# Two stacked feed-forward experts on one core: the planned steps of expert 1 tied to the round ahead of them, chunk 2 joined to the first half of f

## The chip, the cores and the metric

One core of a Trainium2 chip runs the whole program. The metric is the device time of that core in microseconds (us); before the change three runs gave 991.14, 992.07 and 993.05, median 992.07. The profiled execution took 988.78 us, and the span of its trace is 987.0 us.

## The reference, cut to what matters

A two-dimensional DFT (sequence of 3008, width 256) keeps the real part; its 6016 rows go through two feed-forward layers of 2048 hidden units, each without bias:

```python
X = np.fft.fft(np.fft.fft(x, axis=1), axis=2).real      # (2, 3008, 256) -> 6016 rows
h = x @ moe_w_in;  g = h * (1 / (1 + np.exp(-h)))       # expert 1: SiLU
x = g @ moe_w_out
h = x @ moe2_w_in; g = np.maximum(h, 0) + alpha * np.minimum(h, 0)   # expert 2
return g @ moe2_w_out
```

## The kernel before

**Tiling.** A row k of the DFT and its mirrored row -k share their even and odd parts, so each batch is 3 chunks of 502 pairs (CW), 6 chunks in all. A chunk's input is the tile eo (even and odd part, each split into a high and a low fp32r half: product = hi·hi + lo·hi + hi·lo) and n (column 128). Chunks 0 to 2 are batch 0, chunks 3 to 5 batch 1. The 2048 hidden units are 16 slices f of 128.

**Rounds of expert 1.** `ORDER` (L49, L50) lists 96 pairs (chunk, f). Round i (L904 to L909) does, in program order:

- `eo_mm(i)`: 6 matmuls of 502 columns on TensorE into pe and po (L560 to L562); they share four PSUM buffers with the chunk work;
- `mm2(i-2)`: 12 matmuls of the round two back into four accumulators a1 (L608 hi·gh, L610 hi·gl, L612 lo·gh);
- `silu_split(i)`: on VectorE t = n·w + pe (L568), hp = t + po (L571), t = t - po (L572); on ScalarE four SiLUs (L575 gives the rounded gh, L576 the exact value); and `low1(i-1)`, the low halves gl = exact - gh (L588). gl of t is always made on GpSimd; gl of hp on GpSimd in rounds under `LO_POOL` = 17 and in rounds 52 to 87 (`lo_pool`), else on VectorE;
- the steps that `PLAN` puts at round i.

Where the list moves to another chunk, the four accumulators go to the tile o1 of their chunk (L619, L621); the second time a chunk comes, they are added to it (L617).

**Planned steps.** `PLAN` (L26 to L32) gives each piece of other work a range of rounds, and `put` spreads its steps over it: weights of f slices 4 to 15 (`i1`, `i2`, `i3` for w_in, `o0` to `o3` for w_out; f group g needs i*g* at its first `eo_mm` and o*g* at its first `mm2`), chunks 1 and 2 (`c1`, `c2`), the constants `cx` and `fa`, the second batch's first DFT stage (`x` loads, `a` folds and matmuls, `y` loads, `c3` to `c5`), and expert 2's weights (`w2`, `ws`, `wo`, and the coefficients `co` from alpha, L479 to L488, planned at round 60). A weight arrives as float64 bits; one half of 512 columns is converted by one ScalarE step (L181) and four VectorE steps (L185, L189, L193, L197), then summed (L425, L428) and split (L432, L435, L450, L454) on ScalarE and GpSimd.

**What sets the order.** Up to L840 and from L911 the order is as written. In between, a scheduler orders each engine's queue from the program order, the dependences and its own model of the times: where it believes an engine idle, it puts a ready step ahead of the round's work, however late `PLAN` has it. Each engine and the DMA queue (SyncE) then run their queues strictly in order. `tc.issue_after(ins)` binds the instructions traced inside it that are on the engine of `ins` to stand behind `ins` in that queue; it adds no wait between engines. Before the change the steps of `fa`, `o0`, `i1` and `c1` have such a bound (`behind`, L864), the others none.

Expert 2 (from L911) takes 48 steps n of 33 matmuls, in an order that is written out.

Of the kernel before, what the change touches and what calls it, by code (L numbers as in the profile page):

```python
# [15 lines left out]
ALU = mybir.AluOpType  # L16
# [39 lines left out]
A_WARM = (0, 1, 0, 1, 0, 0, 0, 0)  # L56
A_VEC = lambda b, h, i: b and h and i == 0
W2_ORDER = (0, 2, 4, 5, 1, 3, 6, 7)
LO_POOL = 17
K_PARTS = (0, 12, 24, 32)  # L60
B_GROUPS = (0, 3, 6, 9, 12, 16)
PAIRS = [(k0 + i, k0 + (k1 - k0) // 2 + i) for k0, k1 in zip(K_PARTS, K_PARTS[1:]) for i in range((k1 - k0) // 2)]
# [57 lines left out]
def fft_moe_kernel(  # L120
# [294 lines left out]
    def load_o1(g):  # L415
        load_raw(f"o{g}", wo1[:, 1024 * g : 1024 * g + 1024])
# [135 lines left out]
    def eo_mm(i):  # L552
        c, f = ORDER[i]
        g, fo = divmod(f, 4)
        sl = slice(fo * 128, fo * 128 + 128)
        eo = EO[c]
        pe, po = mm_ps(f"pe{i}", CW), mm_ps(f"po{i}", CW)
        for ps, j in ((pe, 0), (po, 2)):
            hi, lo = WI[1, g, j][:, sl], WI[1, g, j + 1][:, sl]
            nc.tensor.matmul(ps, hi, eo[:, j, :], start=True, stop=False)  # L560
            nc.tensor.matmul(ps, lo, eo[:, j, :], start=False, stop=False)  # L561
            LAST["pe"] = nc.tensor.matmul(ps, hi, eo[:, j + 1, :], start=False, stop=True)  # L562
        return pe, po

    def silu_split(i, pe, po):
        c, f = ORDER[i]
        t = work(F32, f"t{i}")
        nc.vector.scalar_tensor_tensor(t, E128[c], w128_sb[:, f : f + 1], pe, op0=ALU.mult, op1=ALU.add)  # L568
        low1(i - 1)
        hp = work(F32, f"hp{i}")  # L570
        nc.vector.tensor_tensor(hp, t, po, op=ALU.add)  # L571
        LAST["t", i] = nc.vector.tensor_tensor(t, t, po, op=ALU.subtract)  # L572
        for s, h in ((0, hp), (1, t)):
            hi = work(F32R, f"gh{i}_{s}")
            nc.scalar.activation(hi, h, AF.Silu)  # L575
# [209 lines left out]
    if True:  # L785
# [99 lines left out]
        put(*PLAN["x"], [lambda j=j: load_x(1, j, 1) for j in range(len(PIECES) - 1)])
        put(*PLAN["a"], a1)
        bs = [stage_b(1, mh) for mh in range(2)]
        for c in range(NCB):
            put(*PLAN[f"y{c}"], [lambda mh=mh, c=c: load_y(1, mh, c) for mh in range(2)])
            put(*PLAN[f"c{3 + c}"], chunk_steps(1, c, bs))  # L890
        a, b = PLAN["w2"]
        for n, j in enumerate(W2_ORDER):
            steps = [lambda j=j: load_w2(j)] + staged([(conv_w2(j, h), []) for h in range(2)])
            put(a + (b - a) * n // 8, a + (b - a) * (n + 1) // 8, steps)
        put(*PLAN["co"], [coefficients])
        for pg in range(2):
            steps = prep_ws(pg)
# [111 lines left out]
```

## Time and profile before

| | us |
|---|---|
| median of 3 runs | 992.07 |
| profiled execution | 988.78 |
| its span | 987.0 |
| PE busy | 957.1 |
| DVE busy | 775.7 |
| ACT busy | 710.4 |
| POOL busy | 405.3 |

PE is TensorE, PEld its weight loads, DVE VectorE, ACT ScalarE, POOL GpSimd, SP SyncE. The stretch to about 30 us is the first DFT stage of batch 0; expert 1 runs from there to about 480 us, expert 2 to the end. PE's ends are modelled, so two neighbouring matmuls overlap on the page; their starts are what tells their pace. PEclk is the share of the full TensorE clock (2.4 GHz) that was granted; 0.5 is 1.2 GHz.

### The profile page before, as it was taken

To read this page: it belongs to the slowest core of one execution; us is meant where nothing else is said; L and a number is where in the kernel's file an instruction comes from. 1 tells how busy PE (TensorE), PEld (TensorE's weight loads), DVE (VectorE), ACT (ScalarE), POOL (GpSimd) and SP (SyncE) were. 2 spreads that over 40 slices of the span, in tenths; PEclk is the share of its full clock that TensorE was granted. 3 is DMA by queue.
4 is the path that set the end of the run, shared out by engine and by line. 5 is a ranking of instruction groups with operands and counts; after the bars stand their busy time and mean duration, and the time that the engine had idled before them with its cause. 6 is when DMAs were issued, how large, how long until landed. Compare 5 with 4: busy or idle time off the path is not lost.

```text
span 987.0 us, 14377 instructions
## 1 busy us (share of the span) xinstructions
PE 957.1 (97%) x5186; PEld 822.9 (83%) x5186; DVE 775.7 (79%) x1328; ACT 710.4 (72%) x1410; POOL 405.3 (41%) x355
## 2 busy tenths in 40 slices
PE   9599899999999999999999999999999999999998
PEld 6478787888888788778789999999999999989997
DVE  6669898785797887777587887878878788787876
ACT  3366666655666766667888888878888788787875
POOL 3577879233347475788441221312213122131200
PEclk9899999999999999999999999999999999999999
DMA  8821100150110120100000000000000000000000
GB/s 276 280 92 59 43 0 1 40 159 1 43 43 2 58 86 1 43 0 1 1 2 22 1 22 22 1 22 1 22 12 11 22 1 22 1 22 22 1 22 21
DMA packets 16614, 37.05 MB, mean 38 GB/s; under 512 B 1824, under 2 KB 11296, under 8 KB 14880
## 3 DMA queue, kind: packets, MB, share of 16 engines
q1 hardware_dynamic: 16544, 36.15, 10.9%
q8 instruction: 40, 0.66, 0.3%
q14 instruction: 30, 0.25, 0.1%
HBM read 26.83 MB, written 9.31 MB: 37 GB/s over the span
## 4 chain that ended last, share of the span: by engine, by line
PE 82%; DVE 6%; POOL 3%; issue 3%; DMA 3%; ACT 2%; SPq 0%; DVEq 0%; POOLq 0%; ACTq 0%
PE a L768 27%; PE ac L670 20%; PE a L610 7%; PE a L608 6%; PE a L612 6%; PE b L670 3%; PE pe L560 2%; PE pe L562 2%; PE po L560 2%; PE pe L561 2%; PE po L562 2%; PE po L561 2%; DMA ys<-ya 2%; PE psa L281 1%; POOL gl L588 1%
## 5 line engine op out<-in xcount | busy, mean ns | idle before, releaser
L768 PE MATMUL a<-gh,wo 128*128 128x502 f32 x768 | 268.4, 391 | 0.0
L588 POOL TENSOR_TENSOR gl<-t,gh 128x502 fp32r<-128x502 f32 x96 | 129.6, 1350 | 91.9 <-ACT t L576 65.4
L768 PEld LDWEIGHTS a<-gh,wo 128*128 128x128 f32 x768 | 145.1, 189 | 23.0
L610 PE MATMUL a<-gl,wo 128*128 128x502 f32 x384 | 150.1, 396 | 10.4 <-POOL gl L588 10.4
L737 DVE SCALAR_TENSOR_TENSOR h<-h,fc,q 128x502 f32<-128x502 f32 x192 | 129.7, 675 | 38.2 <-ACT q L732 35.3
L768 PE MATMUL a<-gl,wo 128*128 128x502 f32 x384 | 149.7, 391 | 0.0
L612 PE MATMUL a<-gh,wo 128*128 128x502 f32 x384 | 148.5, 393 | 0.0
L748 DVE TENSOR_TENSOR gl<-h,gh 128x502 fp32r<-128x502 f32 x192 | 140.7, 733 | 0.1
L575 ACT ACTIVATE gh<-hp 128x502 fp32r<-128x502 f32 x96 | 59.8, 623 | 104.5 <-DVE hp L571 102.1
L608 PE MATMUL a<-gh,wo 128*128 128x502 f32 x384 | 123.7, 397 | 6.4 <-ACT gh L575 6.4
L743 ACT ACTIVATE gh<-h 128x502 fp32r<-128x502 f32 x192 | 118.4, 617 | 2.1 <-DVE h L737 2.1
L732 ACT ACTIVATE q<-h,fc 128x502 f32<-128x502 f32 x192 | 116.9, 609 | 2.9 <-DVE h L715 1.5
L610 PEld LDWEIGHTS a<-gl,wo 128*128 128x128 f32 x384 | 73.0, 190 | 27.7 <-POOL gl L588 13.1
L646 POOL TENSOR_TENSOR xt<-o 128x252 f32<-128x252 f32 x24 | 16.6, 713 | 187.1 <-ACT q L732 131.0
L608 PEld LDWEIGHTS a<-gh,wo 128*128 128x128 f32 x384 | 71.7, 191 | 23.2 <-ACT gh L575 9.4
L588 POOL TENSOR_TENSOR gl<-hp,gh 128x502 fp32r<-128x502 f32 x52 | 68.9, 1324 | 49.2 <-ACT hp L576 44.4
L571 DVE TENSOR_TENSOR hp<-t,po 128x502 f32<-128x502 f32 x96 | 64.5, 672 | 27.2 <-PE po L562 23.7
L568 DVE SCALAR_TENSOR_TENSOR t<-n,sm,pe 128x502 f32<-128x502 f32 x96 | 70.2, 731 | 19.4 <-PE pe L562 16.5
L612 PEld LDWEIGHTS a<-gh,wo 128*128 128x128 f32 x384 | 73.0, 190 | 14.6
L768 PEld LDWEIGHTS a<-gl,wo 128*128 128x128 f32 x384 | 72.6, 189 | 7.7
L704 ACT ACTIVATE u<-ac 128x252 f32<-128x252 f32 x96 | 36.6, 381 | 52.5 <-PE ac L670 52.5
L656 POOL TENSOR_TENSOR os<-o,os 128x252 fp32r<-128x252 f32 x36 | 32.3, 910 | 95.8 <-ACT os L655 92.8
(191 smaller groups left out, 2291.9 us busy)
## 6 DMA issues: line engine op xcount, KB each, us to landing
out_t<-ot SPq DMA_DIRECT2D x24, 251.0 KB, 2.6
x<-in_xs SPq DMA_DIRECT2D x8, 512.0 KB, 5.2
raw_i<-in_wi SPq DMA_DIRECT2D x8, 512.0 KB, 7.5
raw_w<-in_wi SPq DMA_DIRECT2D x4, 1024.0 KB, 6.3
raw_w<-in_wo SPq DMA_DIRECT2D x4, 1024.0 KB, 4.9
raw_o<-in_wo SPq DMA_DIRECT2D x3, 1024.0 KB, 4.9
y<-ys SPq DMA_DIRECT2D x16, 144.0 KB, 3.3
x<-in_xs SPq DMA_DIRECT2D x2, 1024.0 KB, 5.0
```

Of the source, the lines that this page charges most:

```text
L568: nc.vector.scalar_tensor_tensor(t, E128[c], w128_sb[:, f : f + 1], pe, op0=ALU.mult, op1=ALU.add)
L571: nc.vector.tensor_tensor(hp, t, po, op=ALU.add)
L588: (nc.gpsimd if s or lo_pool(i + 1) else nc.vector).tensor_tensor(lo, h, hi.bitcast(F32), op=ALU.subtract)
L608: nc.tensor.matmul(ACC1[lb, s], hi, G[i, s][0], start=st, stop=False)
L610: nc.tensor.matmul(ACC1[lb, s], hi, G[i, s][1], start=False, stop=False)
L612: nc.tensor.matmul(ACC1[lb, s], lo, G[i, s][0], start=False, stop=sp)
L670: nc.tensor.matmul(to, w, x, start=start and q == 0, stop=q == 2, skip_group_check=True)
L732: nc.scalar.activation(h["q", i][:, to], source(n, part), AF.Abs, scale=coef(n, i, 1))
L737: nc.vector.scalar_tensor_tensor(h[f"h{i}"][:, to], source(n, part), coef(n, i, 0), h["q", i][:, to], op0=ALU.mult, op1=ALU.add)
L743: nc.scalar.activation(hi, H[n][f"h{i}"], AF.Copy)
L748: nc.vector.tensor_tensor(lo, H[n][f"h{i}"], G[n, i][0].bitcast(F32), op=ALU.subtract)
L768: nc.tensor.matmul(ACC2[lb], w[lb][j], x, start=st and first, stop=sp and last)
```

## The change

- `behind` goes; `leash(i, steps)` takes its place for all planned steps of round i: each instruction stands, on its engine, behind the last of the round's work: t of round i-1 on VectorE (L572), the gl of round i-2 (L588, on GpSimd), the last SiLU of round i-1 (L576, ScalarE), and the last `eo_mm` matmul of round i-1 (TensorE). SyncE is not bound.
- `ORDER` takes chunks 0, 1 and 2 through f 0 to 7 and then through f 8 to 15; before, chunk 2 ran through all 16 after the other two. f slices 8 to 15 are needed at round 24 and not 16, chunk 2 at round 16 and not 32; and chunk 2's accumulators go out twice (four adds more on VectorE).
- `PLAN` has other rounds, loads of weights, x and `w2` are steps of their own, ahead of their conversions, and `a` comes in four groups of three steps.
- `LO_POOL` is 30: gl of hp moves from VectorE to GpSimd in 13 rounds.

```diff
-    "o0": (1, 2), "i1": (2, 4), "o1": (2, 5), "c1": (2, 6), "i2": (12, 16), "o2": (8, 9), "i3": (16, 18), "o3": (17, 19),
+    "o0": (1, 2), "i1": (1, 4), "o1": (4, 6), "c1": (4, 8), "cx": (8, 9), "c2": (9, 15),
 ...
-ORDER = [(c, f) for f0, f1 in zip(F_PARTS, F_PARTS[1:]) for c in range(2) for f in range(f0, f1)]
-ORDER += [(c, f) for c in range(2, NC) for f in range(NF)]
+ORDER = [(c, f) for f0, f1 in zip(F_PARTS, F_PARTS[1:]) for c in range(NCB) for f in range(f0, f1)]
+ORDER += [(c, f) for c in range(NCB, NC) for f in range(NF)]
 ...
-LO_POOL = 17
+LO_POOL = 30
 ...
-        def behind(st, *at):
+        def leash(i, steps):
+
             with ExitStack() as stack:
-                for k in at:
-                    stack.enter_context(tc.issue_after(LAST[k].ins))
-                run([st])
+                for k in (("t", i - 1), ("gl", i - 2), ("si", i - 1), ("pe", i - 1)):
+                    if k in LAST:
+                        stack.enter_context(tc.issue_after(LAST[k].ins))
+                run(steps)
 ...
         for g in (2, 3):
-            put(*PLAN[f"i{g}"], [lambda g=g: load_w1(g)] + staged(prep_w1(g)))
-            put(*PLAN[f"o{g}"], [lambda g=g: load_o1(g)] + staged(prep_o1(g)))
+            for k, load, prep in (("i", load_w1, prep_w1), ("o", load_o1, prep_o1)):
+                put(*PLAN[f"l{k}{g}"], [lambda load=load, g=g: load(g)])
+                put(*PLAN[f"{k}{g}"], staged(prep(g)))
 ...
-            run(plan.pop(i, []))
+            leash(i, plan.pop(i, []))
```

What the queues hold now, at three places. In the names, gl0_1 is round 0, half 1 (half 0 is of hp, half 1 of t); the last number is a serial; lines after the change are 2 to 4 higher.

GpSimd at the start of the rounds, before: fc is the coefficients (they read alpha's row of sm), wo1_0_1 and wo1_1_1 low halves of w_out.

```order
L454 TENSOR_TENSOR wo1_0_1_292<-cvo0_0_251,wo1_0_0_291 128x512
L483 TENSOR_SCALAR fc_83<-sm_81 128x16
L484 TENSOR_SCALAR fc_83<-sm_81 128x16
L485 TENSOR_SCALAR fc_83<-fc_83 128x16
L454 TENSOR_TENSOR wo1_0_1_292<-cvo0_1_295,wo1_0_0_291 128x512
L486 TENSOR_SCALAR fc_83<-fc_83 128x16
L337 MEMSET z0_2_447 128x4
L487 TENSOR_TENSOR fc_83<-fc_83 128x16
L488 TENSOR_TENSOR fc_83<-fc_83 128x16
L588 TENSOR_TENSOR gl0_0_364<-hp0_345,gh0_0_348 128x502
L588 TENSOR_TENSOR gl0_1_366<-t0_343,gh0_1_351 128x502
```

The same place after the change:

```order
L456 TENSOR_TENSOR wo1_0_1_292<-cvo0_0_251,wo1_0_0_291 128x512
L590 TENSOR_TENSOR gl0_0_364<-hp0_345,gh0_0_348 128x502
L590 TENSOR_TENSOR gl0_1_366<-t0_343,gh0_1_351 128x502
L456 TENSOR_TENSOR wo1_0_1_292<-cvo0_1_295,wo1_0_0_291 128x512
L590 TENSOR_TENSOR gl1_0_415<-hp1_368,gh1_0_371 128x502
L590 TENSOR_TENSOR gl1_1_417<-t1_362,gh1_1_374 128x502
L427 TENSOR_TENSOR we1_436<-cvi1_0_381,cvi1_1_385 128x512
L590 TENSOR_TENSOR gl2_0_460<-hp2_419,gh2_0_422 128x502
L430 TENSOR_TENSOR cvi1_0_381<-cvi1_0_381,cvi1_1_385 128x512
L590 TENSOR_TENSOR gl2_1_462<-t2_413,gh2_1_425 128x502
```

The six coefficient instructions are gone from here (they stand behind gl of rounds 58 and 59), and the second wo1_0_1 is behind both gl of round 0.

VectorE where weight i3 is converted, before (round 12):

```order
L568 SCALAR_TENSOR_TENSOR t12_880<-n0_1_611,sm_81,pe12_860 128x502
L185 TENSOR_SCALAR cvi3_0_1078<-cvi3_0_1078 128x512
L189 TENSOR_SCALAR cvi3_0_1078<-cvi3_0_1078 128x512
L185 TENSOR_SCALAR cvi3_1_1082<-cvi3_1_1082 128x512
L193 SCALAR_TENSOR_TENSOR cvi3_0_1078<-raw_i3_1075,cvi3_0_1078 128x512
L571 TENSOR_TENSOR hp12_886<-t12_880,po12_861 128x502
```

After the change (rounds 19 and 20):

```order
L573 TENSOR_TENSOR hp19_1205<-t19_1199,po19_1180 128x502
L187 TENSOR_SCALAR cvi3_0_1214<-cvi3_0_1214 128x512
L574 TENSOR_TENSOR t19_1199<-t19_1199,po19_1180 128x502
L187 TENSOR_SCALAR cvi3_1_1218<-cvi3_1_1218 128x512
L191 TENSOR_SCALAR cvi3_0_1214<-cvi3_0_1214 128x512
L195 SCALAR_TENSOR_TENSOR cvi3_0_1214<-raw_i3_1011,cvi3_0_1214 128x512
L570 SCALAR_TENSOR_TENSOR t20_1242<-n0_2_1002,sm_81,pe20_1222 128x502
L199 SCALAR_TENSOR_TENSOR cvi3_0_1214<-raw_i3_1011,cvi3_0_1214 128x512
L573 TENSOR_TENSOR hp20_1248<-t20_1242,po20_1223 128x502
```

Four conversion steps stood between t and hp of one round; now one does, and the others stand behind hp.

GpSimd in the last rounds of expert 1 (ws is expert 2's first weight, os0 its split input), before:

```order
L588 TENSOR_TENSOR gl92_1_4322<-t92_4278,gh92_1_4290 128x502
L656 TENSOR_TENSOR os0_1_4295<-xt0_1_4254,os0_0_4294 128x504
L588 TENSOR_TENSOR gl93_1_4365<-t93_4318,gh93_1_4330 128x502
L588 TENSOR_TENSOR gl94_1_4408<-t94_4361,gh94_1_4373 128x502
L588 TENSOR_TENSOR gl95_1_4424<-t95_4404,gh95_1_4416 128x502
```

After the change:

```order
L590 TENSOR_TENSOR gl92_1_4330<-t92_4286,gh92_1_4298 128x502
L523 TENSOR_TENSOR v2w_1_3354<-v2w_1_3354 128x512
L518 TENSOR_TENSOR ws1_5l_4342<-v2w_1_3354,ws1_5h_4341 128x512
L660 TENSOR_TENSOR os0_1_4303<-o1_0_741,os0_0_4302 128x252 x2
L590 TENSOR_TENSOR gl93_1_4373<-t93_4326,gh93_1_4338 128x502
L518 TENSOR_TENSOR ws1_7l_4386<-v2w_1_3354,ws1_7h_4385 128x512
L660 TENSOR_TENSOR os0_1_4303<-xt0_0_4261,os0_0_4302 128x504
L660 TENSOR_TENSOR os0_1_4303<-xt0_1_4262,os0_0_4302 128x504
L590 TENSOR_TENSOR gl94_1_4416<-t94_4369,gh94_1_4381 128x502
L590 TENSOR_TENSOR gl95_1_4432<-t95_4412,gh95_1_4424 128x502
```

Seven steps, most of which stood in earlier rounds, are now between the gl of rounds 92 and 94, where one stood.

## Rows read from the trace of the kernel before

**Rows 1.** The page: busy us (share of the span) and instructions.

```profile
PE 957.1 (97%) x5186; PEld 822.9 (83%) x5186; DVE 775.7 (79%) x1328; ACT 710.4 (72%) x1410; POOL 405.3 (41%) x355
```

**Rows 2.** Windows: stretch, its length, busy us (instructions) by engine, PEclk, DMA.

```profile
30.00:70.00 40.00, 28.72 (x118) 21.98 (x117) 26.32 (x48) 19.62 (x40) 26.03 (x24) 0.87 0.49 168
...
100.00:115.00 15.00, 12.19 (x55) 9.33 (x54) 14.53 (x17) 6.89 (x14) 12.42 (x9) 0.89 0.22 70
...
150.00:170.00 20.00, 19.00 (x81) 14.87 (x80) 18.44 (x24) 13.46 (x24) 20.00 (x22) 1.00 0.00 1
...
285.00:340.00 55.00, 52.88 (x239) 42.40 (x237) 46.09 (x70) 35.42 (x67) 33.55 (x27) 1.00 0.14 46
...
385.00:440.00 55.00, 51.60 (x223) 41.36 (x223) 44.25 (x62) 35.24 (x63) 40.64 (x34) 1.00 0.06 20
...
475.00:500.00 25.00, 22.88 (x138) 19.56 (x137) 14.60 (x29) 21.41 (x47) 12.88 (x12) 1.00 0.00 1
...
500.00:985.00 485.00, 482.51 (x3061) 436.89 (x3060) 388.92 (x744) 390.30 (x820) 98.47 (x97) 1.00 0.04 14
```

**Rows 3.** Timeline of TensorE: start, us, what, [idle before <-releaser].

```profile
46.33 0.79 PE L610 MATMUL a<-gl,wo 128*128 128x502 f32 x1 [7.93 <-POOL gl L588]
...
107.35 1.05 PE L608 MATMUL a<-gh,wo 128*128 128x502 f32 x2 [2.81 <-ACT gh L575]
```

**Rows 4.** Timeline of GpSimd, 39 to 46 us.

```profile
39.14 1.76 POOL L483 TENSOR_SCALAR fc<-sm 128x16 f32<-128x16 f32 x1 [9.25 <-DMA sm<-in_alpha]
...
41.29 3.06 POOL L454 TENSOR_TENSOR wo<-cvo,wo 128x512 fp32r<-128x512 f32 x1
...
45.03 1.24 POOL L588 TENSOR_TENSOR gl<-hp,gh 128x502 fp32r<-128x502 f32 x1
```

**Rows 5.** Windows where the granted clock was lower.

```profile
46.30:52.90 6.60, 6.57 (x20) 5.38 (x21) 2.83 (x4) 3.09 (x6) 3.07 (x3) 0.50 0.69 279
...
107.50:111.00 3.50, 3.50 (x8) 2.16 (x9) 3.50 (x5) 2.36 (x5) 2.97 (x3) 0.51 0.00 0
```

**Rows 6.** Timeline of TensorE at full pace, 467 to 469.4 us.

```profile
467.10 0.39 PE L610 MATMUL a<-gl,wo 128*128 128x502 f32 x1
...
469.38 0.40 PE L612 MATMUL a<-gh,wo 128*128 128x502 f32 x1
```

**Rows 7.** Groups by line and form, VectorE, 30 to 145 us: xcount, busy us, mean ns.

```profile
L568 DVE SCALAR_TENSOR_TENSOR t<-n,sm,pe 128x502 f32<-128x502 f32 x22 | 16.1, 731 | 1.3 <-PE pe L562 0.7 <-POOL gl L588 0.6
L571 DVE TENSOR_TENSOR hp<-t,po 128x502 f32<-128x502 f32 x22 | 14.8, 671 | 5.1 <-PE po L562 3.9 <-PE a L610 0.5
L572 DVE TENSOR_TENSOR t<-t,po 128x502 f32<-128x502 f32 x21 | 14.1, 673 | 0.4
L197 DVE SCALAR_TENSOR_TENSOR cvi<-raw_i,cvi 128x512 uint32<-128x512 uint32 x6 | 7.2, 1206 | 0.0
L193 DVE SCALAR_TENSOR_TENSOR cvi<-raw_i,cvi 128x512 uint32<-128x512 uint32 x6 | 6.9, 1166 | 0.0
...
L189 DVE TENSOR_SCALAR cvi<-cvi 128x512 uint32<-128x512 uint32 x6 | 4.9, 838 | 0.0
L185 DVE TENSOR_SCALAR cvi<-cvi 128x512 f32<-128x512 f32 x6 | 4.3, 728 | 0.1
```

**Rows 8.** Lines L185 and L193: ns least/median/most, first and last start.

```profile
L185 DVE TENSOR_SCALAR cvi<-cvi x8: 412/425/1500, 16.5 to 102.9; 128x512 f32<-128x512 f32 x8
...
L193 DVE SCALAR_TENSOR_TENSOR cvi<-raw_i,cvi x8: 678/691/1747, 17.4 to 108.1; 128x512 uint32<-128x512 uint32 x8
```

**Rows 9.** Timeline of VectorE, 99 to 107 us.

```profile
99.82 0.73 DVE L568 SCALAR_TENSOR_TENSOR t<-n,sm,pe 128x502 f32<-128x502 f32 x1
...
105.98 0.66 DVE L571 TENSOR_TENSOR hp<-t,po 128x502 f32<-128x502 f32 x1
```

**Rows 10.** Timeline of GpSimd, 474 to 479 us.

```profile
474.00 1.28 POOL L588 TENSOR_TENSOR gl<-t,gh 128x502 fp32r<-128x502 f32 x1 [2.46 <-ACT t L576]
477.21 1.28 POOL L588 TENSOR_TENSOR gl<-t,gh 128x502 fp32r<-128x502 f32 x1 [1.93 <-issue]
```

More of the change, by code (lines that the diff above doesn't have):

```diff
@@ L32 @@
 }
+W2_AHEAD = 2
 HALF = 252
@@ L561, in eo_mm @@
             nc.tensor.matmul(ps, lo, eo[:, j, :], start=False, stop=False)
-            LAST["pe"] = nc.tensor.matmul(ps, hi, eo[:, j + 1, :], start=False, stop=True)
+            LAST["pe", i] = nc.tensor.matmul(ps, hi, eo[:, j + 1, :], start=False, stop=True)
         return pe, po
@@ L575, in silu_split @@
             nc.scalar.activation(hi, h, AF.Silu)
-            nc.scalar.activation(h, h, AF.Silu)
+            LAST["si", i] = nc.scalar.activation(h, h, AF.Silu)
             G[i, s] = (hi, h)
@@ L587, in low1 @@
             lo = work(F32R, f"gl{i}_{s}")
-            (nc.gpsimd if s or lo_pool(i + 1) else nc.vector).tensor_tensor(lo, h, hi.bitcast(F32), op=ALU.subtract)
+            LAST["gl", i] = (nc.gpsimd if s or lo_pool(i + 1) else nc.vector).tensor_tensor(
+                lo, h, hi.bitcast(F32), op=ALU.subtract
+            )
             G[i, s] = (hi, lo)
@@ L875, in fft_moe_kernel @@
         put(*PLAN["cx"], [mixed_cosines])
-        put(*PLAN["fa"], [lambda: behind(lambda: split(fh, fl, cs[:, FA0 : FA0 + 128]), 0)])
-        put(*PLAN["o0"], [lambda st=st: behind(st, 0, ("low", 0)) for st in s1[EARLY_O0:] + p1])
-        put(*PLAN["i1"], [lambda st=st: behind(st, 0, ("t", I1_AT)) for st in staged(prep_w1(1))])
+        put(*PLAN["fa"], [lambda: split(fh, fl, cs[:, FA0 : FA0 + 128])])
+        put(*PLAN["o0"], s1[EARLY_O0:] + p1)
+        put(*PLAN["i1"], staged(prep_w1(1)))
         put(*PLAN["o1"], staged(prep_o1(1)))
-        put(*PLAN["c1"], [lambda st=st: behind(st, "pe") for st in chunk_steps(0, 1, (b00, b01))])
+        put(*PLAN["c1"], chunk_steps(0, 1, (b00, b01)))
+        put(*PLAN["c2"], chunk_steps(0, 2, (b00, b01)))
         for g in (2, 3):
-            put(*PLAN[f"i{g}"], [lambda g=g: load_w1(g)] + staged(prep_w1(g)))
-            put(*PLAN[f"o{g}"], [lambda g=g: load_o1(g)] + staged(prep_o1(g)))
-        put(*PLAN["c2"], chunk_steps(0, 2, (b00, b01)))
-        put(*PLAN["x"], [lambda j=j: load_x(1, j, 1) for j in range(len(PIECES) - 1)])
-        put(*PLAN["a"], a1)
+            for k, load, prep in (("i", load_w1, prep_w1), ("o", load_o1, prep_o1)):
+                put(*PLAN[f"l{k}{g}"], [lambda load=load, g=g: load(g)])
+                put(*PLAN[f"{k}{g}"], staged(prep(g)))
+        for j, at in enumerate(PLAN["x"]):
+            put(at, at + 1, [lambda j=j: load_x(1, j, 1)])
+        for j, at in enumerate(PLAN["a"]):
+            put(at, at + 2, a1[3 * j : 3 * j + 3])
         bs = [stage_b(1, mh) for mh in range(2)]
@@ L892, in fft_moe_kernel @@
         for n, j in enumerate(W2_ORDER):
-            steps = [lambda j=j: load_w2(j)] + staged([(conv_w2(j, h), []) for h in range(2)])
-            put(a + (b - a) * n // 8, a + (b - a) * (n + 1) // 8, steps)
+            at, to = a + (b - a) * n // 8, a + (b - a) * (n + 1) // 8
+            put(at - W2_AHEAD, at - W2_AHEAD + 1, [lambda j=j: load_w2(j)])
+            put(at, to, staged([(conv_w2(j, h), []) for h in range(2)]))
         put(*PLAN["co"], [coefficients])
```

5 rows, old and new, of the table PLAN are left out of this document.

## The prediction

> **What bounds the kernel now.** I read the busy times first, then the windows by stretch, then the two longest waits of TensorE, then the queues that ended them. TensorE is busy for 957.1 of 987.0 us [rows 1], and expert 2 leaves nothing to win: from 500 to 985 us it is busy for 482.51 of 485 [rows 2]. So only the idle time of TensorE up to 500 us can go, and the time that it spends at half its clock. The windows put that idle time into six stretches: 40 - 28.72 = 11.28 us between 30 and 70, 2.81 between 100 and 115, 1.00 between 150 and 170, 2.12 between 285 and 340, 3.40 between 385 and 440, 2.12 between 475 and 500 [rows 2]; 22.7 in all. Twice the granted clock was 0.5, its lower level of 1.2 GHz, after TensorE had stood still: while it worked for 6.57 us behind the first long wait and for 3.5 us around the second [rows 5]; half of that, 3.3 and 1.7 us, is lost. Together 27.7 us, of which the start of expert 2 (2.1) is written out by hand and not touched.
>
> The first long wait is 7.93 us, for a gl of round 0 [rows 3]. GpSimd, which makes it, stood 9.25 us for alpha's transfer in front of a coefficient that nobody needs before round 60, then did a half of w_out for 3.06 us, and only at 45.03 the gl [rows 4]. The second is 2.81 us, for a SiLU [rows 3]: VectorE began t of that round at 99.82 and hp at 105.98 [rows 9], with the four conversion steps between them that the order shows. In both, a planned step whose round lies later stands in a queue ahead of the round's own work. That is what the change forbids.
>
> **The change, part by part.** All sums are made against the profiled execution (988.78 us, 1.78 over its span); the median of the runs is 3.3 above it, and the gain is carried over to the median.
>
> *The start (30 to 70 us).* At stake are 11.28 idle and 3.3 of slow clock, 14.6 us. After the change the coefficients are no longer in front of gl, so GpSimd waits for no transfer there. What is late next is VectorE. Up to round 7 it does 8 x (0.731 + 0.671 + 0.673) = 16.6 us of t, hp and t, and the four halves of i1 and o1, each 0.728 + 0.838 + 1.166 + 1.206 = 3.94 us [rows 7], 15.8 in all: 32.4. TensorE has in the same rounds 48 matmuls of eo_mm, 72 of mm2 up to round 5 and 10 of chunk 1; ten matmuls took 469.38 - 467.10 = 2.28 us [rows 6], so 130 take 29.6. VectorE is behind by 2.8. GpSimd's queue holds 13 steps up to the gl of round 3, at some 1.26 us [rows 4, 10] 16.4 us, exactly what four rounds of 18 matmuls take: it can't catch up its late start, for which I take 2.2 (of t, hp and gl of round 0 alone, 2.6 us and the SiLUs between them, part lies beside the first eo_mm), and I add 1.4 for rounds 1 to 3, where a weight step of about 1.3 us stands ahead of a gl. That keeps 6.4 of 14.6: gain 8.2. Bounds: all 14.6; or a loss of 2, worked out under the second rival.
>
> The waits that stay are near one us each, and the clock fell only behind one of eight and one of three; so I count no slow clock there. If it falls nevertheless for as long as before, 3.3 come off.
>
> *The conversions of i2, i3, o2, o3 (100 to 115).* At stake 2.81 + 1.7 = 4.5. In the new order one conversion step stands between t and hp, not four, and the next stand behind hp, where the SiLUs hide them. I keep 0.5: gain 4.0. Bounds 0 and 4.5.
>
> *The first stage of batch 1 (150 to 170).* The folds came as one bunch; now each piece has three rounds. But two folds of 512 columns still stand behind one gl, and GpSimd was busy for all 20 us of this stretch [rows 2]. Half of the 1.0: gain 0.5, bounds 0 and 1.
>
> *Expert 2's weights (285 to 440).* At stake 2.12 + 3.40 = 5.5 of idle, the same pattern as at 100. There are 16 halves over 38 rounds, now one to four steps a round, mostly behind t or hp. VectorE's load stays: it was busy for 44.25 of 55 us [rows 2], so not every bunch can be spread. I keep 1.0: gain 4.5; bounds 5.5 and, if the steps spread over every round hold up each a little, -3.
>
> *The end of expert 1.* Between gl of rounds 92 and 94 GpSimd now has seven steps, three of them short, near 8 us, instead of one of 1.3. Before, it stood idle for 2.46 and 1.93 us here [rows 10], which covers 4.4 of the 6.7 more. The rest, 2.3, makes gl of round 94 late; its matmul comes two rounds later. I take a loss of 0.7; bounds 0 and 2.3.
>
> *Work moved.* 13 gl leave VectorE for GpSimd, four adds come for chunk 2's second exit; both lie beside a round's 4.1 us of matmuls on TensorE. GpSimd pays 13 x 1.28 us there, in rounds 17 to 29, where it has room; without that cover up to 1 us. The loads as own steps stand on SyncE, two to five rounds ahead of their readers: cost nothing, since a round is 4.1 us; a load that came late would hold VectorE's or ScalarE's head, which is the third rival.
>
> Sum: 8.2 + 4.0 + 0.5 + 4.5 - 0.7 = 16.5 us. The execution would take 972.3, the median 992.07 - 16.5 = **975.6**.
>
> *A rule against it.* VectorE's conversion steps take far longer in some places: 412 ns at least and 1500 at most for one, 678 and 1747 for another [rows 8]; and the four between t and hp of rows 9 filled 105.98 - 99.82 - 0.73 = 5.4 us. The Trainium skill, GPSIMD Engine Reference, section 1 (Specifications), says that GpSimd shares its SBUF interfaces with VectorE and that VectorE's instructions with two SBUF inputs or in a two-port mode contend with it. The trace agrees by the spread just named. By that rule alone a change that spreads conversions over rounds in which GpSimd is always at work, and moves 13 gl to it, makes VectorE slower; that is the second rival.
>
> **Rivals.**
>
> *Nearly all of it goes.* For it: the order after the change has no bunch left between t and hp, and waits under a matmul's length are hidden in the modelled ends, so more than 27.7 may be at stake. Against: VectorE's 32.4 us at the start. Then 14.6 + 4.5 + 1.0 + 5.5 = 25.6: 966.5.
>
> *VectorE slows beside GpSimd.* At the dearest price a half costs 1.5 + 1.5 + 1.75 + 1.75 = 6.5 us (rows 8's most, taken for the other two steps as well) and not 3.94; four halves cost 10.2 more, and the start loses 2. Half-way to it the start gains 3.1, and if the other gains are halved (4.5), less 0.7, 6.9 stay: 985.2. For it: the spread of rows 8, and GpSimd's queue without a gap at the start. Against: the medians, 425 and 691 ns, lie at the low end.
>
> *Slower: heads of queues.* A conversion's first step is now bound behind the last SiLU of the round before; the next, on VectorE, waits for it, and t of the next round waits behind that. There are 28 halves behind round 0. It decides at 16.5 / 28 = 0.6 us lost on TensorE for each; at 1.2 us each, one step's time [rows 7], it is 33.6 - 16.5 = 17 us slower: 1009. A load that lands late acts the same way. For it: the queue of 39 us in rows 4 was just this, one waiting head. Against: in the new order VectorE's step stands a round behind ScalarE's, so its input is there.
>
> **How the numbers follow.** The forecast (971 to 981) has 0.54, nearly all gone (under 971) 0.18, VectorE slower (981 to 990) 0.20, no change 0.03, slower 0.05. The range 966 to 987 leaves out a little at the low end and, above, the rest of the second rival, no change and slower: about 0.16. A measurement of this kernel tells some 0.2% (2 us) from no change; so faster 0.92, same 0.03, slower 0.05.
>
> **What would show it.** Right: no wait of GpSimd for in_alpha, the coefficients near 300 us; no stretch at clock 0.5 between 30 and 70 and idle time of TensorE there of about 6; TensorE idle under 0.5 where i2 and i3 are converted and about 1 where the weights of expert 2 are; hp within about 1.5 us of the end of t where weights are converted. Wrong: conversion steps with means over 1.2 us throughout the rounds; VectorE idle at a conversion step until ScalarE; slow clock in a new place; a DMA as the releaser of any wait of ScalarE or GpSimd behind round 0.

## The result, and the profile after

The changed kernel takes 977.07 us (median of four runs, 975.78 to 978.35), the kernel before beside it 992.37; the ratio is 0.9847, 95% interval 0.9828 to 0.9866. The forecast was 975.6. The profiled execution took 975.78 us with a span of 974.0: 13.0 less than before in both, where the sum had 16.5. The kernel before has its longest median in this set; the later sets have 989.66 to 991.11.

The page's first line and windows by stage answer to [rows 1, 2]:

```profile
PE 953.6 (98%) x5186; PEld 821.7 (84%) x5186; DVE 785.1 (81%) x1319; ACT 709.3 (73%) x1410; POOL 424.6 (44%) x368
```

```profile
30.00:70.00 40.00, 34.17 (x138) 25.35 (x137) 35.29 (x50) 22.91 (x44) 25.89 (x21) 0.91 0.52 175
70.00:115.00 45.00, 44.77 (x204) 37.03 (x204) 34.98 (x51) 31.07 (x57) 33.48 (x31) 1.00 0.14 48
115.00:160.00 45.00, 45.00 (x198) 36.74 (x197) 40.40 (x54) 31.07 (x56) 38.54 (x29) 1.00 0.00 1
160.00:200.00 40.00, 39.59 (x173) 32.35 (x172) 31.57 (x44) 25.41 (x44) 29.78 (x25) 1.00 0.08 27
200.00:285.00 85.00, 83.92 (x390) 69.69 (x389) 66.93 (x100) 50.18 (x95) 37.31 (x35) 1.00 0.24 70
285.00:340.00 55.00, 55.00 (x252) 45.82 (x252) 45.97 (x72) 38.36 (x72) 38.59 (x37) 1.00 0.14 46
...
385.00:440.00 55.00, 55.00 (x243) 45.35 (x242) 50.83 (x67) 40.47 (x73) 43.92 (x32) 1.00 0.06 20
440.00:490.00 50.00, 45.87 (x245) 38.31 (x244) 33.89 (x54) 41.31 (x86) 37.88 (x34) 1.00 0.00 1
```

Read the third column against the second. From 285 to 440 us, where expert 2's weights are converted, TensorE now loses nothing; i2, i3, o2 and o3 (70 to 160) cost 0.23 us at full clock. Idle time is left at the start (5.83), between 200 and 285 (1.08) and at the end of expert 1 (4.13). In the same places the kernel before had, beside the 11.28 and 2.12 of [rows 2], none:

```profile
170.00:285.00 115.00, 115.00 (x525) 95.89 (x525) 86.34 (x132) 70.21 (x128) 39.09 (x34) 1.00 0.17 52
...
440.00:475.00 35.00, 35.00 (x156) 29.09 (x155) 26.26 (x37) 25.76 (x45) 28.27 (x24) 1.00 0.00 1
```

GpSimd's timeline (start, us, what, idle before) answers to [rows 4]. No transfer stands in front of the first gl, only the work of round 0 itself, and the coefficients run at 306 us:

```profile
35.62 1.27 POOL L590 TENSOR_TENSOR gl<-hp,gh 128x502 fp32r<-128x502 f32 x1 [5.35 <-ACT hp L578]
...
306.42 0.19 POOL L485 TENSOR_SCALAR fc<-sm 128x16 f32<-128x16 f32 x1
```

TensorE's waits at the start answer to [rows 3], the windows of lower clock to [rows 5]:

```profile
45.86 0.72 PE L612 MATMUL a<-gh,wo 128*128 128x502 f32 x2 [1.22 <-ACT gh L577]
47.65 0.71 PE L612 MATMUL a<-gh,wo 128*128 128x502 f32 x2 [1.07 <-ACT gh L577]
48.82 0.79 PE L562 MATMUL pe<-eo,wi 128*128 128x502 f32 x1 [0.46 <-ACT wi L434]
...
57.91 0.49 PE L562 MATMUL pe<-eo,wi 128*128 128x502 f32 x1 [1.86 <-DVE z L347]
```

```profile
48.70:52.11 3.41, 3.29 (x8) 2.69 (x9) 0.41 (x2) 3.38 (x8) 3.41 (x5) 0.50 0.65 243
58.94:62.35 3.41, 3.19 (x8) 2.59 (x9) 3.38 (x8) 2.13 (x4) 0.84 (x1) 0.50 0.02 5
```

The wait of 7.93 us is gone, but the clock still went to its lower level twice, for 6.82 us in all. VectorE's timeline shows what stood ahead of the SiLUs of the first two waits, and then what made the wait of 1.86:

```profile
42.20 2.36 DVE L195 SCALAR_TENSOR_TENSOR cvi<-raw_i,cvi 128x512 uint32<-128x512 uint32 x2
44.48 0.67 DVE L573 TENSOR_TENSOR hp<-t,po 128x502 f32<-128x502 f32 x1
...
52.08 0.94 DVE L187 TENSOR_SCALAR cvo<-cvo 128x512 f32<-128x512 f32 x1 [3.00 <-ACT cvo L183]
53.05 1.39 DVE L191 TENSOR_SCALAR cvo<-cvo 128x512 uint32<-128x512 uint32 x1
54.36 1.49 DVE L187 TENSOR_SCALAR cvo<-cvo 128x512 f32<-128x512 f32 x1
55.77 1.73 DVE L195 SCALAR_TENSOR_TENSOR cvo<-raw_o,cvo 128x512 uint32<-128x512 uint32 x1
57.42 0.44 DVE L347 TENSOR_TENSOR z<-psb,z 128x282 fp32r<-128x282 f32 x1
```

Round 2 still has conversion steps of i1 inside its own work: three between t (40.58) and hp (44.48), two more before its second t (46.27); the bound holds them behind round 1 only. Near 52 us VectorE stood 3.00 us in front of o1's first step, whose ScalarE step is bound behind the SiLUs; then four conversion steps ran for 5.5 us, and chunk 1's z (L347, the low half of a DFT result, read out of PSUM; round 5's first matmul waited for it) stood behind them. The end of expert 1 on GpSimd, and the TensorE wait that came of it:

```profile
452.88 1.30 POOL L523 TENSOR_TENSOR v2w<-v2w 128x512 f32<-128x512 f32 x1
454.13 1.75 POOL L518 TENSOR_TENSOR ws_5l<-v2w,ws_5h 128x512 fp32r<-128x512 f32 x1
455.84 1.33 POOL L660 TENSOR_TENSOR os<-o,os 128x252 fp32r<-128x252 f32 x2
457.11 1.30 POOL L590 TENSOR_TENSOR gl<-t,gh 128x502 fp32r<-128x502 f32 x1
458.35 1.75 POOL L518 TENSOR_TENSOR ws_7l<-v2w,ws_7h 128x512 fp32r<-128x512 f32 x1
460.06 2.93 POOL L660 TENSOR_TENSOR os<-xt,os 128x504 fp32r<-128x504 f32 x2
462.95 2.46 POOL L590 TENSOR_TENSOR gl<-t,gh 128x502 fp32r<-128x502 f32 x2
```

```profile
464.24 0.49 PE L614 MATMUL a<-gl,wo 128*128 128x502 f32 x1 [1.68 <-POOL gl L590]
```

GpSimd works without a gap from 452.88 on, and its seven steps took 9.1 us (rows above, without the gl between them); gl of round 94 starts at 462.95, 4.5 us after that of round 93 ended.

### The profile page after: what moved, and what is told of

Its sections match the earlier page's. It is cut to its first block, busy times and chain, and to the rows that moved or that the text cites. A ratio compares the mean times of both kernels' runs of the same rounds, so it can differ in the third digit from the quotient of the medians.

```text
span 974.0 us, 14393 instructions
## 1 busy us (share of the span) xinstructions
PE 953.6 (98%) x5186; PEld 821.7 (84%) x5186; DVE 785.1 (81%) x1319; ACT 709.3 (73%) x1410; POOL 424.6 (44%) x368
## 4 chain that ended last, share of the span: by engine, by line
PE 87%; DVE 3%; POOL 3%; ACT 3%; issue 2%; DMA 0%; SPq 0%; POOLq 0%; DVEq 0%; ACTq 0%
PE a L772 27%; PE ac L674 20%; PE a L614 7%; PE a L616 7%; PE a L612 7%; PE b L674 3%; PE po L562 2%; PE po L564 2%; PE pe L562 2%; PE po L563 2%; PE pe L564 2%; PE pe L563 2%; POOL gl L590 2%; PE psb L327 1%; PE psa L283 1%
## 5 line engine op out<-in xcount | busy, mean ns | idle before, releaser
L772 PE MATMUL a<-gh,wo 128*128 128x502 f32 x768 | 268.2, 391 | 0.0
L590 POOL TENSOR_TENSOR gl<-t,gh 128x502 fp32r<-128x502 f32 x96 | 133.6, 1392 | 55.4 <-ACT t L578 44.5
L616 PE MATMUL a<-gh,wo 128*128 128x502 f32 x384 | 146.6, 392 | 0.0
L612 PE MATMUL a<-gh,wo 128*128 128x502 f32 x384 | 119.2, 393 | 2.4 <-ACT gh L577 2.3
L590 POOL TENSOR_TENSOR gl<-hp,gh 128x502 fp32r<-128x502 f32 x65 | 90.1, 1386 | 68.1 <-ACT hp L578 66.5
L616 PEld LDWEIGHTS a<-gh,wo 128*128 128x128 f32 x384 | 73.1, 190 | 14.6
```

Source lines behind the costliest of these rows:

```text
L590: LAST["gl", i] = (nc.gpsimd if s or lo_pool(i + 1) else nc.vector).tensor_tensor(lo, h, hi.bitcast(F32), op=ALU.subtract)
L612: nc.tensor.matmul(ACC1[lb, s], hi, G[i, s][0], start=st, stop=False)
L616: nc.tensor.matmul(ACC1[lb, s], lo, G[i, s][0], start=False, stop=sp)
L772: nc.tensor.matmul(ACC2[lb], w[lb][j], x, start=st and first, stop=sp and last)
```

## The experiments

Two theories of the 13 us. A: what stood in an in-order queue ahead of a round's own work made the loss, and the bound takes it away. B: the new plan makes the gain (chunk 2 joined, weights later, loads ahead). Ratios are to the kernel before, run beside each kernel; rows with different values under "before" come from different sets, so between them the ratios are what compares.

| run | median us | before | ratio (95%) |
|---|---|---|---|
| coefficients late, alone | 987.36 | 990.31 | 0.9961 (0.9947 to 0.9976) |
| bound alone | 980.22 | 990.31 | 0.9894 (0.9881 to 0.9907) |
| changed, no bound | 1002.17 | 990.31 | 1.0119 (1.0102 to 1.0136) |
| changed, o1 earlier | 975.60 | 990.31 | 0.9851 (0.9834 to 0.9867) |
| changed, again | 977.59 | 991.11 | 0.9869 (0.9852 to 0.9886) |
| changed, split earlier | 974.10 | 991.11 | 0.9829 (0.9813 to 0.9844) |
| changed, chunk 1 earlier | 973.40 | 991.11 | 0.9825 (0.9808 to 0.9841) |
| changed, LO_POOL 17 | 977.63 | 991.11 | 0.9866 (0.9849 to 0.9883) |
| split and chunk 1 two rounds earlier | 973.37 | 990.02 | 0.9834 (0.9812 to 0.9855) |
| split and chunk 1 earlier | 973.44 | 990.02 | 0.9831 (0.9808 to 0.9855) |
| changed, half the conversions of i1, o1 | 972.79 | 990.02 | 0.9826 (0.9803 to 0.9850) |
| changed, GpSimd alone bound | 987.07 | 989.66 | 0.9971 (0.9961 to 0.9981) |

**Coefficients late, alone** (kernel before).

```diff
-        put(*PLAN["co"], [coefficients])
+        put(*PLAN["co"], [lambda: behind(coefficients, ("gl", 58))])
```

> The kernel before, with one thing moved: the six coefficient instructions on GpSimd stand behind the gl of round 58. Theory A (what stands in a queue ahead of a round's own work is the cause, alpha's wait first, but not alone): the 7.93 us wait of TensorE for gl goes and with it the slow clock behind it; VectorE keeps its conversion steps between t and hp of rounds 0 and 1 and becomes the next; 5 to 10 us faster than before, 982 to 987; the wait of 2.81 us near 107 us, and those between 285 and 440 us, stay. Theory B (alpha's wait was hidden behind VectorE, which is full in the first rounds): under 2 us, 990 or more. Theory C (alpha's wait is nearly the whole gain of the change): 13 us or more, 979 or less.

It gained 3.9 us by the ratio (2.4 to 5.2 by its interval), at or below the low end of theory A and far from theory C. The execution with the trace was the longest of its twelve (990.04; span 988.2, 1.2 more than before), so the rows show where the waits went and not the gain. TensorE's windows and waits at the start of this kernel:

```profile
30.00:70.00 40.00, 31.80 (x126) 24.63 (x125) 30.93 (x50) 21.65 (x43) 23.05 (x19) 0.87 0.51 170
```

```profile
44.54 0.73 PE L610 MATMUL a<-gh,wo 128*128 128x502 f32 x2 [1.70 <-ACT gh L575]
47.14 1.60 PE L325 MATMUL psb<-cs,y 96*128 96x94 f32 x6 [1.86 <-DVE z L345]
```

The one wait of 7.93 us became several of 1.3 to 1.9, all of them for VectorE or for a SiLU behind it; idle time went from 11.28 to 8.20 us and the mean clock stayed at 0.87. Alpha's transfer covered VectorE's queue, which was nearly as late.

**Bound alone** (kernel before, `leash` in place of `behind`).

```diff
-            run(plan.pop(i, []))
+            leash(i, plan.pop(i, []))
```

> The kernel before, with the bound alone: every planned step behind the round ahead of it on each engine, but the old order of chunks, the old rounds of the plan and LO_POOL 17. Theory A (the order in the queues makes the gain): more than half of it, 977 to 984; GpSimd doesn't wait for in_alpha, the wait near 107 us and those between 285 and 440 us are under 1 us in all, and the start keeps a wait because the old plan puts i1, o1 and chunk 1 into the same rounds 2 to 5 (eleven VectorE instructions between t and hp of round 3). Rival (the plan makes it: chunk 2 joined, weights later, loads ahead): less than half, 985 to 992.

It has 10.5 us by the ratio (0.0106 of 990), the larger part of the change's gain. Its windows:

```profile
30.00:70.00 40.00, 32.94 (x140) 24.63 (x139) 34.25 (x51) 23.71 (x46) 24.66 (x20) 0.91 0.58 193
...
115.00:150.00 35.00, 30.84 (x117) 22.09 (x116) 33.34 (x46) 21.18 (x38) 20.33 (x15) 0.95 0.00 1
```

From 285 to 440 us TensorE loses nothing, as in the changed kernel. The start has 1.2 us more idle time than there, and where the old plan puts i3, o3 and chunk 2 together (115 to 150) VectorE is full, 33.34 of 35 us, and TensorE loses 4.16. This second place is what the new plan spreads out. Which part of the rest of the change (the joined chunk, the rounds, the loads as own steps) brings how much was not run; LO_POOL alone was, below.

**Changed, no bound.**

```diff
-            leash(i, plan.pop(i, []))
+            run(plan.pop(i, []))
```

> The changed kernel without the bound: the new order of chunks, plan and LO_POOL, but the scheduler may put a planned step ahead of a round's work. The coefficients are then in front of the gl of round 0 again, and i1, o1 and i2 between t and hp of rounds 0 to 2. Theory A (the queues' order): no gain or a loss, 988 to 1000, with a wait for in_alpha of GpSimd and a first wait of TensorE above 5 us. Rival (the plan makes the gain): 977 to 984.

It is slower than before, a little past the end of theory A's range; theory B falls: without any bound the new plan loses 12 us. This run also lacks the four bounds that the kernel before had (on `fa`, `o0`, `i1` and `c1`); the new plan with those old bounds was not run, so the 12 us are the price of no bound at all. GpSimd stands for alpha again:

```profile
38.33 0.20 POOL L485 TENSOR_SCALAR fc<-sm 128x16 f32<-128x16 f32 x1 [8.65 <-DMA sm<-in_alpha]
```

TensorE's waits at the start are at most 2.9 us, though, not over 5: as in the first run, VectorE is late too and divides the wait.

**Changed, GpSimd alone bound.**

```diff
-                for k in (("t", i - 1), ("gl", i - 2), ("si", i - 1), ("pe", i - 1)):
+                for k in (("gl", i - 2),):
```

> The changed kernel with the bound on GpSimd alone: VectorE, ScalarE and TensorE are free again, so that i1 and o1 stand between t and hp of rounds 0 to 2 as without any bound, while alpha and the weight steps of GpSimd stay behind gl. Without any bound it was 1002, with all four 977.5. Theory A (VectorE's conversion steps ahead of a round's own t and hp are the larger part): less than half of the 24 us comes back, 990 to 1000. Rival (GpSimd's queue is the larger part, as the longest wait of the kernel before was for gl): more than half, 978 to 989.

Theory A's division was wrong: 15 of the 24.6 us between no bound (1002.17) and the whole bound (977.59) come back with GpSimd's bound alone (0.0148 of 0.0250 by the ratios). The other 9.5 belong to the bounds on VectorE, ScalarE and TensorE together, which were not run one by one. TensorE's longest wait is now for a SiLU:

```profile
51.22 0.73 PE L612 MATMUL a<-gh,wo 128*128 128x502 f32 x2 [2.55 <-ACT gh L577]
```

**Changed, o1 earlier.**

```diff
-"o1": (4, 6)
+"o1": (3, 6)
```

> The changed kernel with o1 planned a round earlier (rounds 3 to 5 and not 4 and 5): ScalarE's two first steps of o1 then stand ahead of the SiLUs of round 3, and chunk 1's z stands behind six conversion steps of which the first can start some 3 us earlier. Theory A (the wait of 1.86 us for z and the second stretch at clock 0.50, 3.4 us, come from VectorE standing 3.0 us for ScalarE in front of o1's first step): both go, 2 to 3.6 us faster than the changed kernel, 973.5 to 975. Rival (VectorE is simply full in the first eight rounds, 35.3 of 40 us): the wait moves to another place, within 1 us of the changed kernel, 976 to 978.

No difference to the changed kernel that the intervals show; the wait for z stood at 58.03 with 1.83 us. VectorE's timeline, then ScalarE's:

```profile
49.77 2.59 DVE L187 TENSOR_SCALAR cvo<-cvo 128x512 f32<-128x512 f32 x2 [0.28 <-ACT cvo L183]
...
57.52 0.45 DVE L347 TENSOR_TENSOR z<-psb,z 128x282 fp32r<-128x282 f32 x1 [0.99 <-ACT z L345]
```

```profile
56.56 0.63 ACT L452 ACTIVATE wo<-cvo 128x512 fp32r<-128x512 f32 x1 [3.68 <-DVE cvo L199]
```

The 3 us of standing are gone, but six conversion steps (49.77 to 56.5 us) and not four now ran ahead of z on VectorE, and on ScalarE a step of o1 stood 3.68 us for them, in front of z's own. Moving one piece ahead only changed which queue z stood in; to take the standing at o1's first step away did not take the wait for z away.

**Changed, again**, to compare with the next three.

> The changed kernel as it is, a second time, as the measure for the others of this set: 976 to 979. In its trace the two stretches at clock 0.50 (near 49 and 59 us), the wait of 1.9 us for z and that of 1.7 us for gl near 464 us stand again if the order causes them, and not if they were chance.

The same waits stand at 47.53 (1.06), 57.80 (2.29) and 463.76 (1.68): they come of the order. The slow clock does not quite: two stretches of 3.41 us stand near 47 and 58 us as before, but a third, near 464 us, is in this trace and not in the first, behind the same wait of 1.68.

**Changed, split earlier.**

```diff
-        put(n1 - 5, n1 - 1, split_o1(0))
+        put(n1 - 9, n1 - 5, split_o1(0))
```

> The changed kernel with the split of expert 2's first input (the L650 and L660 steps on GpSimd) planned at rounds 87 to 90 and not 91 to 94, so that only three steps of weight 1 stand between the gl of rounds 92 and 94. Theory A (GpSimd's queue at the end of expert 1 costs 2.0 us: idle time of TensorE from 440 us on grew from 2.12 to 4.14): the wait of 1.7 us for gl goes, 1.5 to 2 us faster than the changed kernel beside it, and no wait comes up near 430 us. Rival (the same steps then hold up the gl of rounds 86 to 91, or the wait of 1.6 us for e that expert 2 has anyway takes the time): within 0.7 us of the changed kernel.

3.5 us faster than the changed kernel beside it; more than expected:

```profile
440.00:490.00 50.00, 46.90 (x249) 39.05 (x247) 36.43 (x58) 41.35 (x85) 37.37 (x31) 1.00 0.00 1
```

```profile
451.71 0.49 PE L614 MATMUL a<-gl,wo 128*128 128x502 f32 x1 [1.00 <-POOL gl L590]
```

Idle time there is 3.10 and not 4.13; the wait is smaller and came earlier. In the run beside it the clock also fell behind the wait of 1.68 us (mean 0.97 from 440 to 490 us, here 1.00): 1.0 of idle and half of some 3 us make the 2.5 between the spans, 975.0 and 972.5. Against the first trace of the changed kernel, where the clock did not fall there, the spans differ by 1.5 (974.0 and 972.5).

**Changed, chunk 1 earlier.**

```diff
-"c1": (4, 8)
+"c1": (3, 7)
```

> The changed kernel with chunk 1 planned at rounds 3 to 6 and not 4 to 7: its first z then stands ahead of o1's conversion steps on VectorE and on ScalarE, where o1 a round earlier had left it behind them. Theory A (the wait for z is the place of z in two queues, not VectorE's load): the wait of 1.9 us and the second stretch at clock 0.50 go, 2.5 to 4 us faster than the changed kernel beside it; only the first stretch, near 49 us, stays. Rival (VectorE is full, 35.3 of 40 us from 30 to 70, whatever stands first): o1's weights come later by what z came earlier, another wait of 1 to 2 us and slow clock behind it, within 1 us of the changed kernel.

4.2 us faster, and still the wait for z stood at 57.50 with 2.25 us (now the second half's z) and both stretches of slow clock: the time is near theory A's, the reason not. From 30 to 70 us TensorE was busy for 35.82 us and not 34.46, which is 1.4 of the 4.2; another 1.7 is the third slow stretch of the run beside it, 400 us later, which this trace doesn't have and which the edit is not shown to have removed. What went are the waits for gh (1.07) and wi (0.46): chunk 1's matmuls now fill those places.

**Split and chunk 1 earlier**: both edits.

> The changed kernel with both single edits: chunk 1 at rounds 3 to 6, the split of expert 2's first input at rounds 87 to 90. They lie 400 us apart: the gains of 4.2 and 3.5 us add, 969 to 971; the wait of 2.3 us for z near 57 us stays, that for gl near 460 us is 1.0 or less. Rival (the runs of the changed kernel beside them were a little long and the gains hold some of that): 971 to 973.

Half a us beyond the rival's end: the gains don't add. Its trace has both falls of idle time (busy 35.84 us from 30 to 70, 46.91 of 50 from 440 to 490); but each single gain was taken against the repeat, whose trace has the third slow stretch, and that can go only once. One trace of each kernel fits this reading; it is not shown for the medians. This version, like either edit alone, is faster than both kernels (973.4 to 974.1). Its ratio is 0.0016 below that of the changed kernel in the first set and 0.0038 below the repeat, 1.6 to 3.8 us; the intervals overlap, so its size stays loose.

**Split and chunk 1 two rounds earlier.**

```diff
-"c1": (3, 7)
+"c1": (2, 6)
```

> The changed kernel with the split of expert 2's first input at rounds 87 to 90, as in the run before it, and chunk 1 at rounds 2 to 5: all four of its z groups then stand ahead of o1's conversion steps, where the chunk a round earlier had still left the second half's behind them. Theory A (the order of z and o1 on VectorE makes the wait of 2.3 us near 57 us, and the slow clock behind it): that wait goes, and the gains of the two single edits (4.2 and 3.5 us beside the changed kernel) add up with about 2 us more: 967 to 970. Rival (what helped was only that chunk 1's matmuls came where TensorE stood idle, and VectorE's load sets the end of the stretch): the gains add, but the wait only moves, 969.5 to 971.5.

Above both ranges, and not faster than the run before. Its window and two longest waits:

```profile
30.00:70.00 40.00, 33.47 (x151) 25.42 (x150) 36.22 (x52) 24.02 (x47) 24.78 (x20) 1.00 0.58 190
```

```profile
38.41 0.88 PE L327 MATMUL psb<-cs,y 96*128 96x94 f32 x6 [1.34 <-DMA y<-ys]
...
59.70 0.50 PE L562 MATMUL pe<-eo,wi 128*128 128x502 f32 x1 [2.76 <-DVE eo L168]
```

The clock was whole throughout, and TensorE's idle time rose from 4.16 us in the run before to 6.53. Of the 2.4 more, 1.34 is a wait for the load of y, which chunk 1 now asks for before it has landed; the rest fits the rival, that VectorE (busy 36.22 of 40 us) sets the end of the stretch, and is not shown apart from it.

**Changed, half the conversions of i1, o1.**

```diff
-        return box, [zero, one, two, three, four]
+        return box, [zero, three, four] if n in ("i1_0", "i1_1", "o1_0", "o1_1") else [zero, one, two, three, four]
```

> The changed kernel without two of the four VectorE steps (L187, L191) of the four halves of i1 and o1, so that their weights are wrong: eight VectorE instructions fewer in the first rounds, some 9 us by their means. Theory A (VectorE's load, with the order of its queue, is what still holds TensorE up from 30 to 70 us: 5.8 us idle and two stretches of 3.4 us at clock 0.50): idle time there falls under 3 us and at least one stretch goes, 4 to 8 us faster than the changed kernel, 969 to 973. Rival (ScalarE's steps or the loads of the weights come so late that they would hold TensorE up as much): within 2 us of the changed kernel.

4.3 us against the repeat by the ratio (0.9869 to 0.9826), which is within theory A's range, but 2.1 against the first set (0.9847), which is under it; the changed kernel was not run beside this one. Both slow stretches are gone, the idle time is 4.10 us and not under 3:

```profile
30.00:70.00 40.00, 35.90 (x160) 27.22 (x159) 30.95 (x45) 24.91 (x48) 30.50 (x26) 1.00 0.51 171
```

**Changed, LO_POOL 17.**

```diff
-LO_POOL = 30
+LO_POOL = 17
```

> The changed kernel with LO_POOL 17 as before: 13 gl of hp, in rounds 17 to 29, on VectorE and not on GpSimd. Theory A (GpSimd's 13 gl lie beside other work and cost nothing, and the conversion steps that they slow are hidden): within 1.5 us of the changed kernel; the means of the conversion steps from 104 to 155 us, 0.76 to 1.32 us, come down as GpSimd works less. Rival 1 (they slow VectorE and TensorE waits for it): faster by 2 us or more. Rival 2 (gl between t and hp is what held TensorE up): slower by 2 us or more, with waits for gh in that stretch.

Theory A: the same time. Two of VectorE's eight groups of conversion steps from 104 to 155 us, in the changed kernel and then in this one (count, busy us, mean ns):

```profile
L195 DVE SCALAR_TENSOR_TENSOR cvi<-raw_i,cvi 128x512 uint32<-128x512 uint32 x2 | 2.3, 1172 | 0.1
L199 DVE SCALAR_TENSOR_TENSOR cvi<-raw_i,cvi 128x512 uint32<-128x512 uint32 x2 | 2.3, 1164 | 0.0
```

```profile
L195 DVE SCALAR_TENSOR_TENSOR cvi<-raw_i,cvi 128x512 uint32<-128x512 uint32 x2 | 2.5, 1226 | 0.0
...
L199 DVE SCALAR_TENSOR_TENSOR cvi<-raw_i,cvi 128x512 uint32<-128x512 uint32 x2 | 1.4, 686 | 0.0
```

With 13 gl fewer on GpSimd (busy 23.31 and not 38.54 us from 115 to 160) six of the eight groups became shorter, L199 on cvi from 1164 to 686 ns, while L195 on cvi did not; together they fell from 22.1 to 17.8 us, and the end does not move.

## Why the prediction was right, and where it was not

By terms, from the windows (idle time plus half of the time at clock 0.50):

| term | forecast | measured |
|---|---|---|
| start | 8.2 | 14.6 - 5.83 - 3.41 = 5.4 |
| i2, i3, o2, o3 | 4.0 | 4.5 - 0.23 = 4.3 |
| batch 1's first stage | 0.5 | 1.0 - 0.41 = 0.6 |
| expert 2's weights | 4.5 | 5.5 - 0.59 = 4.9 |
| end of expert 1 | -0.7 | 2.12 - 4.13 = -2.0 |
| work moved | 0 | -0.5 |

That is 12.7 where the sum had 16.5. It is not the whole account of the 13.0 between the spans: up to 30 us, before any round, TensorE was busy 26.00 us and not 27.62 (1.6 lost), and 0.1 net came from the stretches that no term names. That leaves some 11; the other 2 lie in TensorE's busy time (957.1 and 953.6, of which the clock explains 1.6 of 3.5), whose ends are modelled, and no row places them. The stretch up to 30 us lies between 25.66 and 27.92 over the twelve experiments, so the 1.6 may be chance; why it varies stays open.

The order of the queues was the right mechanism, as the bound alone and the run without it show. The closeness of the number is in part luck: the forecast median, 975.6, is 1.5 from the measured 977.07, because the kernel before was long in that set (15.3 us between the medians). The repeat shows 13.5 and the two traces 13.0; the forecast of 16.5 is above all three.

*The start.* That VectorE is late next is shown. The step that failed is "The waits that stay are near one us each ... so I count no slow clock there": two stretches of 3.41 us cost 3.4 us, nearly the 3.3 that the text names for this case. The clock fell at 48.70, after waits of 1.22 and 1.07 and in one of 0.46, and at 58.94, 1.0 us after one of 1.86. The idle time of 5.83 is near the 6.4 that was kept, but its parts are not: 2.8 were for VectorE and 3.6 for GpSimd, and TensorE waited some 4.4 us (1.22, 1.07, 1.86, 0.29) for VectorE or a SiLU behind it, 0.9 for a gl of GpSimd and 0.5 for a weight step of ScalarE. The 2.2 for GpSimd's late start did not come up: no wait of TensorE stands between 36 and 41 us. That the sum of the parts is right is luck.

*The signs.* Two signs of being right failed and two of being wrong came up. Slow clock stood between 30 and 70 us, the second time in a new place. VectorE stood at a conversion step for ScalarE seven times, 0.40 to 3.00 us and 9.2 in all. That is the third rival's mechanism, but the only long wait of TensorE behind one of them is the 1.86 for z, and a wait for z stayed when o1 a round earlier took that standing away; what makes this wait is not shown further than that VectorE's work is part of it. The argument "VectorE's step stands a round behind ScalarE's" does not hold where ScalarE's own step stands behind SiLUs. And hp did not keep within about 1.5 us of the end of t where weights are converted: it came 2.9 us after it at 106.84, behind two steps of o2, and 3.1 at 368.95, where the longest before were 5.4 and 5.9; from 70 to 115 us TensorE lost at most 0.23 us by it, from 340 to 385 nothing.

*The other gains.* Where four to six conversion steps stood between t and hp, at most two do now behind the start, and next to no wait is left where weights are converted. The loads as own steps cost nothing: no wait of TensorE, VectorE, ScalarE or GpSimd behind round 0 is released by a DMA.

*The end of expert 1* has the mechanism named, at the far end of its bounds (2.3). The seven steps took 9.1 us and not "near 8", and "its matmul comes two rounds later" gave too much cover.

*Work moved* was priced at nothing. The four adds of chunk 2's second exit (L621) stand on VectorE around a gl of hp, three of them ahead of it, and TensorE waited 0.49 us for that gl at 265.18. A second wait for a gl of hp, 0.59 us at 274.45, has another cause: expert 2's first weight is being converted, a step of it stands between t and that gl, and the gl itself took 1.76 us; it is in the table with the weights. VectorE between 261 and 274 us, then TensorE:

```profile
261.37 0.68 DVE L621 TENSOR_TENSOR o<-a,o 128x502 f32<-128x502 f32 x1
...
262.60 1.26 DVE L621 TENSOR_TENSOR o<-a,o 128x502 f32<-128x502 f32 x2
263.78 1.35 DVE L590 TENSOR_TENSOR gl<-hp,gh 128x502 fp32r<-128x502 f32 x1
...
272.64 1.76 DVE L590 TENSOR_TENSOR gl<-hp,gh 128x502 fp32r<-128x502 f32 x1
```

```profile
265.18 0.50 PE L614 MATMUL a<-gl,wo 128*128 128x502 f32 x1 [0.49 <-DVE gl L590]
...
274.45 0.50 PE L614 MATMUL a<-gl,wo 128*128 128x502 f32 x1 [0.59 <-DVE gl L590]
```

*The second rival's* premise came true in part and decided little: the 132 conversion steps (L187, L191, L195, L199) took 117.7 us in all and 101.3 before, and VectorE's busy time rose by 9.4 us although 13 gl left it and only four adds came. The Trainium skill, GPSIMD Engine Reference, section 1 (Specifications), has VectorE's instructions with two SBUF inputs, or in a two-port mode, contend with GpSimd for the SBUF interfaces that they share; here L199 on cvi, with two SBUF inputs, took 686 or 1164 ns by what GpSimd did beside it. But means over 1.2 us throughout did not come up (0.77 to 0.99 by line over the whole kernel), and TensorE waits for such steps only at the start and once near 274 us.

## What to carry to other kernels

Bind filler work behind the round's own work on every in-order engine; the same plan with no bound at all was 12 us slower than the kernel before. Such a bound holds filler work behind the round before, not behind the round it is planned in: in round 2 here three steps still stood between t and hp. When one long wait is traced to one cause, ask which queue is the next late one before its whole length is counted: removing alpha's wait alone gave 3.9 us. Before single gains are added up, ask whether the run that they were measured against had a stretch of slow clock that each of them counts. And where another engine is nearly full, as VectorE was at the start, moving one piece ahead may only move the wait; here less work on that engine (with steps left out), or other matmuls in the gaps, went with a faster kernel.

## What the runs showed of the hardware

The granted clock fell to 0.50, 1.2 GHz, after waits of 1.22 and 1.07 us (in one of 0.46) and again after one of 1.86, for 3.41 us each time. After the same wait of 1.68 us near 464 us it fell in one execution of the changed kernel and not in another, and in another kernel it stayed at 1.00 after one of 2.76. The length of one wait does not tell whether it falls.

VectorE's instructions that read PSUM kept their time everywhere (t took 719 to 740 ns in the two kernels, hp 660 to 681), while a conversion step with SBUF operands alone took 412 to 1500 ns [rows 8]; with less work on GpSimd six of eight groups of them became shorter, L199 on cvi from 1164 to 686 ns.
